# Attention into a mixture of experts on one core: which DMA engines carry the rows of one weight, and how the output's first tiles are split

## The chip, the core and the metric

The kernel runs on one core of a Trainium2 chip. The core has TensorE (PE) for matrix products, VectorE (DVE) and ScalarE (ACT) for elementwise work, GpSimd (POOL) and SyncE (SP), which issue transfers here, and sixteen DMA engines that move the data. The metric is the time of one execution on the device in microseconds. Times are medians over runs; a profiled execution gives the details.

## The reference

Attention over 4 batches of 8 heads (768 positions, 64 columns), with a causal mask that in some heads keeps only the first 4 positions and a window of 64. Its output, as 3072 rows of 512, goes through a soft mixture of 8 experts with 4 slots each:

```python
a = softmax(where(mask, q @ k.T / 8, -1e9)); x = a @ v      # 3072 x 512 over all heads
logits = x @ phi                                           # 3072 x 32
d = exp(logits) / sum over rows; slot_input = d.T @ x      # 32 x 512
for e in range(8):
    slot_out[e] = maximum(slot_input[e] @ w1[e], 0) @ w2[e]
c = exp(logits) / sum over slots
out = c @ slot_out                                         # 3072 x 512, float32
```

Inputs and output are float32; the kernel works in bfloat16 between them. The sixteen weights (eight w1, eight w2) are 2 MB each in float32.

## The kernel before

The instruction order comes from a planner that is part of the kernel: `pl.op` registers an operation with the engines that may run it, an estimated duration, a due time and what it depends on, and `pl.run()` places all operations in one order from these; each engine's queue holds its operations in that order. What the planner thinks of durations has no part in the time on the chip except through the order.

**Loads.** All of q, k, v and all weights (except a first slice of weight 0, and phi) are loaded by GpSimd (`dma`, line 281; the issue is line 283), with a cast from float32 to bfloat16 on the way. The order of the loads is written out by hand (line 901). A load waits for the landing of the load eight places before it. A weight takes a tile of 128 partitions; one row of it, 4096 numbers, is 16 KB in DRAM and 8 KB in the tile. Weight 5 is `UNEVEN` (line 355): it is loaded in five pieces of 112, 5, 5, 5 and 1 rows, each issued in turn. It lies in the middle of the load order, before the last parts of q, k and v and the ten weights after it. The last weight, number 15, is loaded in two halves of 256 columns each, `w15a` and `w15b`, so that the work on the first half can begin before the second is there.

**The tail.** After attention, the products with w1 (`H`, line 945) and w2 (`W2`, line 990) follow each other as the weights land. The products of the last w2 are done for columns 0 to 255 (`W2.7`, when `w15a` is there) and later for columns 256 to 511 (`W2.8`, when `w15b` is there). The accumulated slots are scaled by the reciprocal of a sum: `SOa` (line 1008) writes the first half, on ScalarE, `SOc` copies it on GpSimd into the tile that holds both halves, and `SOb` (line 1013) writes the second half; it may go to ScalarE or VectorE, and the planner puts it on ScalarE.

**The output.** It has 24 tiles of 128 rows by 512 columns (six groups `gi` of four, `r`). Each needs one product with the slots (`OM`, line 1056), and one scaling from PSUM into SBUF (`OE`, lines 1064 on ScalarE and 1066 on VectorE). The first six tiles (`half`, line 1044) are split by columns: their first halves need only `SOa` and are made while `w15b` is still being loaded, alternately on ScalarE and VectorE; their second halves need `SOb`. The remaining eighteen are made whole. The early products take turns on four PSUM banks. An extra dependency (lines 1073 to 1077) keeps `W2.8` behind the last early product in TensorE's queue.

**The stores.** SP issues eleven stores in the order of `store_parts` (line 1078): the first halves of tiles 0.0-0.1, 0.2-0.3 and 1.0-1.1, the second halves of the same, then tiles 1.2-1.3 whole, then four groups of four tiles (1 MB each). A store waits for the scalings of its tiles. A store of half tiles moves rows of 1 KB, the store of tiles 1.2-1.3 rows of 4 KB, the stores of groups rows of 8 KB.

Of the kernel before, what the change touches and what calls it, by code (L numbers as in the profile page):

```python
# [15 lines left out]
ACT = mybir.ActivationFunctionType  # L16
# [157 lines left out]
def kernel(  # L174
# [76 lines left out]
    def tr_bf(s, n):  # L251
# [17 lines left out]
    pl = Plan({"S8": 11, "QT": 2, "KT": 2, "VT": 1, "VB": 2, "VF": 3, "PT": 2, "PTX": 2, "XB": 2,  # L269
               "XT": 1, "SC": 2, "TR": 2, "PV": 1})  # L270
# [10 lines left out]
    def dma(name, key, nbytes, ndesc, buf, dst, src, deps=()):  # L281
        iss = pl.op("issue " + name, {"POOL": 0.62}, key, deps=deps, acq=[buf] if buf else [], lead=1.3,
                    emit=lambda o: nc.gpsimd.dma_start(dst(), src))  # L283
        issues.append(iss)
        gen = pl.op("gen " + name, {"GEN": 2.5 if name[0] == "w" and int(name[1:3].rstrip("abc")) > 5 else 1.45}, key, deps=[iss])
        land = pl.op("land " + name, {"DMA": dma_us(nbytes, ndesc) + LATE.get(name, 0.0)}, key, deps=[gen], lead=3.3)
        ring.setdefault(name, []).append((iss, land))
        return land

    def dma_us(nbytes, ndesc):  # L290
        return ndesc / 16 * 0.004 + nbytes / 16 / RATE
# [40 lines left out]
    def w_view(i):  # L332
        m = late_mem[i]() if i in late_mem else slots[wbuf[i].slot][:, :]
        return m.rearrange("p (a f) -> p a f", a=4 if i < NE else 8)

    def load_w(i, key, deps=()):
        if i == 0:

            flat = lambda: w_view(0).rearrange("p a f -> p (a f)")
            wland[0] = dma("w0", key, 7 << 18, 128, wbuf[0], lambda: flat()[:, WF:],  # L340
                           moe_w1[0].rearrange("(di do) f -> di (do f)", do=4)[:, WF:])
            w_cast.append(pl.op("CW", {"ACT": 0.6}, -90, deps=[wf_land], need=[wbuf[0]],
                                emit=lambda o: nc.scalar.copy(flat()[:, 0:WF], wf)))
            return
        if i < NE:
            src = moe_w1[i].rearrange("(di do) f -> di do f", do=4)
        else:
            src = moe_w2[i - NE].rearrange("(fi fo) d -> fi fo d", fo=8)
            if i == NW - 1:
                for k, (c0, c1) in enumerate(((0, CH), (CH, 512))):  # L350
                    last_lands.append(dma(f"w15{'ab'[k]}", key + 0.1 * k, (c1 - c0) << 12, 1024, None,
                                          lambda c0=c0, c1=c1: w_view(i)[:, :, c0:c1], src[:, :, c0:c1], deps=deps))
                wland[i] = last_lands[0]
                return
        if i == UNEVEN:

            buf, prev, land = wbuf[i], [], []
            for p0, p1 in ((0, 112), (112, 117), (117, 122), (122, 127), (127, 128)):
                land.append(dma(f"w{i}", key, (p1 - p0) << 14, p1 - p0, None if prev else buf,
                                lambda p0=p0, p1=p1: w_view(i)[p0:p1], src[p0:p1], deps=prev))  # L360
                prev = [issues[-1]]
            wland[i] = pl.op(f"landed w{i}", {"SP": 0.01}, key, deps=land)
            return
        wland[i] = dma(f"w{i}", key, 2 << 20, 128, None if i in late_mem else wbuf[i],
                       lambda: w_view(i), src, deps=deps)
# [151 lines left out]


    load_w(0, -30)
    for x in "ABC":  # L520
        load_tile(x, -29)
    load_w(1, -28)
    load_w(2, -27)
    for x in "DE":
        load_tile(x, -26)
# [103 lines left out]
    def evs(x, b, n):  # L629
        if b == 0:  # L630
            return ev[x, b]
        return [e for r0, r1, e in ev[x, b] if r0 < 24 * (n + 1) and r1 > 24 * n]
# [33 lines left out]
    for b in range(B):  # L666
        for n in range(4):
# [30 lines left out]
            for kk, g in enumerate(GORDER):  # L698
                sc = Buf("SC")
                key = k0 + kk * T / 5.3  # L700
# [17 lines left out]
                if g in (1, 3, 4):  # L718
                    m = {1: 0, 3: 1, 4: 2}[g]
                    masko[p, m] = pl.op(f"MK.{p}.{m}", {"DVE": [0.70, 0.70, 0.57][m]}, key + 0.3,  # L720
                                        deps=[expo[p, x] for x in ((0, 1), (2, 3), (3, 4))[m]] + o_hm[n],
                                        emit=mask_emit(b, n, m))

        for ns in ([(0, 1), (2, 3)] if b == 0 else [(0, 1, 2, 3)]):
            sc = Buf("SC")

            def emit_lx(o, b=b, sc=sc, ns=ns):
                sc_mms(sc, b, [(128 * x, n, XJ, XI, 1) for x, n in enumerate(ns)])

            key = T * (4 * b + ns[0]) + 0.9 * T  # L730
            a = pl.op(f"QX.{b}.{ns[0]}", {"PE": 0.09 * len(ns)}, key - 2.0, n=2 * len(ns),
                      deps=list(dict.fromkeys(e for n in ns for x in "qk" for e in evs(x, b, n))),
# [15 lines left out]
    for b in range(B):  # L748
        for n in range(4):
# [5 lines left out]
            for i in iorder:  # L755
                deps, need = [v2e[p], vfo[p]], set()
# [6 lines left out]
                def emit_pv(o, b=b, n=n, p=p, i=i):  # L763
                    pT = pTs[PTb[b, n].slot]
                    vb = vbs[VBb[b].slot]
                    for h in range(2):
                        for j in range(i + 1):
# [3 lines left out]
                            else:  # L771
# [5 lines left out]
                             deps=list(dict.fromkeys(deps)) + ([last] if last else []),  # L777
                             acq=[PVb[p]] if i == 0 else [],
                             rel=[PTb[b, n]] + ([VFb[p]] if i == 5 else []) +
# [72 lines left out]
        def emit_sa(o, b=b, dp=dp):  # L852
# [5 lines left out]
            else:  # L858
# [7 lines left out]
                       rel=[dp], emit=emit_sa)  # L866
# [47 lines left out]
    kt = T * 16 + 10  # L914
# [19 lines left out]
    hse, hte, w2o = {}, {}, []  # L934

    for e4 in range(2):
        hse[e4] = []
        for c in range(2):
# [13 lines left out]
            def emit_hr(o, e4=e4, c=c, bank=bank):  # L952
# [3 lines left out]
                else:  # L956
# [3 lines left out]
                                 rel=[hp], emit=emit_hr))  # L960
# [14 lines left out]
    so = Buf("PV")  # L975
# [26 lines left out]
    def emit_so(o, d, c0, c1):  # L1002
        if o.eng == "ACT":
            nc.scalar.activation(d[:, c0:c1], pvb[:, 0, c0:c1], ACT.Copy, scale=rcs[:, 0:1])  # L1004
        else:
            nc.vector.tensor_scalar(d[:, c0:c1], pvb[:, 0, c0:c1], rcs[:, 0:1], None, op0=ALU.mult)
# [3 lines left out]

    so_c = pl.op("SOc", {"POOL": 0.4}, kt + 20, deps=[so_a],
                 emit=lambda o: nc.gpsimd.tensor_copy(slot_out[:, 0:CH], slot_out_a[:, 0:CH]))
    so_b = pl.op("SOb", {"ACT": 0.46, "DVE": 0.49}, kt + 29.0, deps=[w2o[-1], so_c], rel=[so],
                 emit=lambda o: emit_so(o, slot_out, CH, 512))

    def emit_gz(o):
# [23 lines left out]
    def ot_view(gi):  # L1040
        return slots[wbuf[gi].slot].bitcast(F32)[:, :].rearrange("p (r d) -> p r d", r=4)

    oe, tiles = {}, [(gi, r) for gi in range(6) for r in range(4)]
    half = tiles[:6]
    parts = [(gi, r, 0, CH) for gi, r in half] + [(gi, r, CH, 512) for gi, r in half] + \
        [(gi, r, 0, 512) for gi, r in tiles[6:]]
    for m, (gi, r, d0, d1) in enumerate(parts):
        early = d0 == 0 and d1 == CH
        c = ("SC", "TR")[m % 2] if early else ("SC", "TR", "PV", "SC", "TR")[(m - len(half)) % 5]
# [5 lines left out]
        def emit_om(o, gi=gi, r=r, d0=d0, d1=d1, bank=bank, early=early):  # L1055
# [3 lines left out]
                  deps=[so_a if early else so_b], acq=[bf], emit=emit_om)  # L1059

        def emit_oe(o, gi=gi, r=r, d0=d0, d1=d1, bank=bank):
# [3 lines left out]
            else:  # L1065
                nc.vector.tensor_scalar(d, bank(), sc_, None, op0=ALU.mult)  # L1066

        w = (d1 - d0) / 512
# [7 lines left out]
    y.ndep += 1  # L1076
    x.succ.append(y)
    store_parts = [(gi, r0, r1, d0, d1) for d0, d1 in ((0, CH), (CH, 512)) for gi, r0, r1 in
                   ((0, 0, 2), (0, 2, 4), (1, 0, 2))] + [(1, 2, 4, 0, 512)] + [(gi, 0, 4, 0, 512) for gi in range(2, 6)]
    for n, (gi, r0, r1, d0, d1) in enumerate(store_parts):  # L1080
        def emit_st(o, gi=gi, r0=r0, r1=r1, d0=d0, d1=d1):
            dst = out[512 * gi:512 * (gi + 1), :].rearrange("(p r) d -> p r d", r=4)
# [25 lines left out]
    for o in order:  # L1108
# [9 lines left out]
        if front:  # L1118
# [3 lines left out]
            n = int(0.75 * (gap - 0.1) / unit + 0.5) if gap > 0.2 else 0  # L1122
# [23 lines left out]
        us, w = gap - (1.5 if o.name[:2] == "W2" else 0.12), 512 - c0  # L1146
# [53 lines left out]
```

## Time and profile before

| | us |
|---|---|
| median of 3 runs (range) | 148.75 (148.67 to 149.09) |
| profiled execution, whole time | 148.61 |
| its span, first to last instruction | 146.84 |
| PE, DVE, ACT busy in the span | 125.4, 111.6, 110.3 |
| load queue (q0), share of 16 engines over the span | 88.8% |

The times in the profile count from the first instruction of the span. "Busy" is the time in which an engine's instructions ran. The profile's DMA share is the mean busy share of the sixteen DMA engines; it can come out a little above 1 where the records of packets overlap. A load or a store is split into packets that the sixteen engines work through; each engine reports its part of a transfer as complete on its own, and the transfer has landed with the sixteenth report.

### The profile page before, as it was taken

How to read it: one execution, taken by the hardware profiler on the slowest of the kernel's cores; microseconds unless marked ns; L12 is line 12 of the kernel's file. 1: busy time of each engine (PE TensorE's matmuls, PEld its weight loads, DVE VectorE, ACT ScalarE, POOL GpSimd, SP SyncE). 2: the span in 40 equal slices, each digit the busy share in tenths (PEclk: the TensorE clock that was granted, in tenths of full speed). 3: DMA queues.
4: the chain of work that ended last, by engine and by line, in shares of the span. 5: the costliest groups of instructions: out<-in, count | busy, mean ns of one | idle time of the engine just before them, and what ended most of it. 6: DMA issues, size and time to landing. Idle time of an engine off the chain costs nothing.

```text
span 146.8 us, 4972 instructions
## 1 busy us (share of the span) xinstructions
PE 125.4 (85%) x2171; PEld 80.9 (55%) x2171; DVE 111.6 (76%) x244; ACT 110.3 (75%) x143; POOL 24.0 (16%) x48
## 2 busy tenths in 40 slices
PE   6999899989899998999999999998778996679200
PEld 2365566668576675877576776765534564233000
DVE  3898399987999899899999999999847610249500
ACT  3374999989999999999998999999814700469600
POOL 6921110412011211110400211010700000100000
PEclk9999999999999999999999999999999999968955
DMA  4999999999999999999999999999999999979996
GB/s 100 190 214 215 225 204 211 218 210 228 214 206 212 215 223 214 219 214 203 211 216 224 212 214 219 216 216 214 214 219 214 216 215 186 137 246 392 413 415 250
DMA packets 9608, 33.03 MB, mean 225 GB/s; under 512 B 867, under 2 KB 4595, under 8 KB 7283
## 3 DMA queue, kind: packets, MB, share of 16 engines
q0 software_dynamic: 6912, 26.09, 88.8%
q1 hardware_dynamic: 2672, 6.62, 11.8%
q8 instruction: 17, 0.28, 0.7%
q14 instruction: 5, 0.04, 0.1%
q10 hardware_dynamic: 2, 0.00, 0.0%
HBM read 52.49 MB, written 6.29 MB: 400 GB/s over the span
## 4 chain that ended last, share of the span: by engine, by line
DMA 33%; PE 23%; DVE 15%; ACT 14%; POOL 4%; issue 4%; ACTq 0%; POOLq 0%
DMA slot<-in_v_dram 17%; DMA qk<-in_moe_w_dram 16%; ACT pt L713 9%; PE pv L773 7%; PE sc L641 6%; DVE pt L658 4%; DVE xv L787 3%; POOL slot L283 3%; PE tr L611 3%; DVE qk L278 2%; ACT slot L1064 2%; PE tr L799 2%; DVE xT L278 2%; PE tr L676 2%; PE sc L1056 1%
## 5 line engine op out<-in xcount | busy, mean ns | idle before, releaser
L713 ACT ACTIVATE pt<-sc 128x1024 bf16<-128x1024 f32 x80 | 76.8, 1045 | 3.0 <-PE sc L641 2.5
L641 PE MATMUL sc<-qk 64*128 64x512 bf16 (+3 forms) x256 | 31.2, 308 | 2.7 <-ACT pt L713 1.8
L658 DVE TENSOR_TENSOR pt<-pt,msk 128x1024 bf16<-128x1024 bf16 (+1 forms) x48 | 30.0, 640 | 0.5 <-ACT pt L713 0.4
L773 PEld LDWEIGHTS <-pt 128*128 128x128 bf16 x640 | 23.4, 97 | 6.7 <-issue 5.6
L773 PE MATMUL pv<-vx,pt 128*128 128x65 bf16 x352 | 26.1, 193 | 0.1
L773 PE MATMUL pv<-vf,pt 128*128 128x65 bf16 x288 | 20.9, 194 | 0.0
L641 PEld LDWEIGHTS <-qk 64*128 64x128 bf16 x256 | 10.3, 93 | 11.5 <-issue 4.5
L611 PE MATMUL tr<-ident,slot 128*64 128x128 bf16 (+1 forms) x448 | 15.5, 219 | 0.5 <-DMA slot<-in_v_dram 0.5
L787 DVE TENSOR_TENSOR xv<-pv,rs 128x768 bf16<-128x768 f32 x16 | 15.3, 957 | 0.6
L611 PEld LDWEIGHTS <-slot 128*64 128x64 bf16 (+1 forms) x448 | 12.7, 110 | 3.6 <-issue 3.2
L283 POOL DMA_DIRECT2D slot<-in_moe_w_dram x15 | 8.1, 541 | 39.8 <-PE tr L611 9.1
L278 DVE COPY qk<-tr 128x768 bf16<-128x768 bf16 (+2 forms) x24 | 12.9, 551 | 0.7 <-PE tr L611 0.4
L278 DVE COPY xv<-tr 128x768 bf16<-128x768 bf16 (+2 forms) x20 | 8.4, 432 | 2.9 <-PE tr L569 2.9
L799 PE MATMUL tr<-ident,xv 128*128 128x128 bf16 x96 | 8.1, 220 | 2.2 <-DVE xv L787 1.9
L278 DVE COPY xT<-tr 128x768 bf16<-128x768 bf16 x14 | 7.8, 554 | 1.0 <-PE tr L799 0.8
L1004 ACT ACTIVATE msk<-pv,rcs 128x256 bf16<-128x256 f32 x2 | 0.9, 474 | 10.0 <-PE pv L990 10.0
L799 PEld LDWEIGHTS <-xv 128*128 128x128 bf16 x96 | 5.7, 97 | 4.7 <-DVE xv L787 2.2
L1066 DVE TENSOR_SCALAR slot<-tr,rrow 128x256 f32<-128x256 f32 (+1 forms) x6 | 3.3, 571 | 6.5 <-PE tr L1056 6.4
L676 PE MATMUL tr<-ident,xv 128*128 128x128 bf16 x96 | 7.9, 220 | 0.1
L278 DVE COPY vx<-tr 128x768 bf16<-128x768 bf16 x14 | 7.7, 550 | 0.2 <-PE tr L676 0.2
L1157 PE MATMUL pv<-zero 128*128 128x512 bf16 x30 | 7.5, 382 | 0.0
L692 DVE TENSOR_TENSOR vf<-vx,fm 128x528 bf16<-128x528 bf16 x16 | 6.9, 430 | 0.3
(122 smaller groups left out, 172.3 us busy)
## 6 DMA issues: line engine op xcount, KB each, us to landing
slot<-in_moe_w_dram POOLq DMA_DIRECT2D x9, 1024.0 KB, 22.8
out_dram<-slot SPq DMA_DIRECT2D x4, 1024.0 KB, 5.9
slot<-in_q_dram POOLq DMA_DIRECT2D x3, 768.0 KB, 20.0
slot<-in_k_dram POOLq DMA_DIRECT2D x3, 768.0 KB, 15.1
slot<-in_moe_w_dram POOLq DMA_DIRECT2D x2, 896.0 KB, 23.1
slot<-in_v_dram POOLq DMA_DIRECT2D x2, 768.0 KB, 13.2
out_dram<-slot SPq DMA_DIRECT2D x6, 256.0 KB, 2.5
slot<-in_v_dram POOLq DMA_DIRECT2D x2, 512.0 KB, 24.2
```

Source lines behind the costliest of these rows:

```text
L278: nc.vector.tensor_copy(dst, src)
L283: emit=lambda o: nc.gpsimd.dma_start(dst(), src))
L611: nc.tensor.transpose(t[64 * i:64 * (i + 1), :, s, :], rv[:, i, 8 * c + s, :], ident[0:nr, 0:nr])
L641: nc.tensor.matmul(scb[sc.slot][:, i, c:c + 128 * nb], kk, qq.rearrange("p b c -> p (b c)"), start=True, stop=True)
L658: nc.vector.tensor_tensor(pw, pw, mw, op=ALU.mult)
L676: nc.tensor.transpose(t[:, 128 * j:128 * (j + 1)], vT[:, 6 * n + j, :], ident)
L692: nc.vector.tensor_tensor(vfs[VFb[p].slot], vv, fm[:, n], op=ALU.mult)
L713: nc.scalar.activation(pTs[PTb[b, n].slot][:, :, 512 * g:512 * (g + 1)], scb[sc.slot], ACT.Exp, scale=scale)
L773: nc.tensor.matmul(pvb[:, h, 65 * i:65 * (i + 1)], lt, rhs, start=(j == 0), stop=(j == i))
L787: nc.vector.tensor_tensor(xo, pvw[:, :, :, 0:64], r.rearrange("p i (j o) -> p i j o", o=1).to_broadcast([P, 2, 6, 64]), op=ALU.mult)
L799: nc.tensor.transpose(t[:, 128 * i:128 * (i + 1)], xv[:, i, 128 * n:128 * (n + 1)], ident)
L1157: nc.tensor.matmul(bank[:, c0:c0 + w], zero[:, 0:128], zero[:, 0:w], start=(c0 == 0), stop=True, skip_group_check=True)
```

## The change

Two things are changed. Weight 5 is loaded in pieces of 96, 8, 8, 8 and 8 rows; the second piece takes 8 consecutive rows (96 to 103), the last three take every third row from 104, 105 and 106 on. And the output's first seven tiles, instead of six, are split by columns; the third and the sixth store now hold three half tiles each (1.0 to 1.2), and the seventh store holds tile 1.3 alone. `SOb` may only go to VectorE.

```diff
         if i == UNEVEN:

             buf, prev, land = wbuf[i], [], []
-            for p0, p1 in ((0, 112), (112, 117), (117, 122), (122, 127), (127, 128)):
-                land.append(dma(f"w{i}", key, (p1 - p0) << 14, p1 - p0, None if prev else buf,
-                                lambda p0=p0, p1=p1: w_view(i)[p0:p1], src[p0:p1], deps=prev))
+            for p0, p1, st in ((0, 96, 1), (96, 104, 1), (104, 128, 3), (105, 128, 3), (106, 128, 3)):
+                n = len(range(p0, p1, st))
+                land.append(dma(f"w{i}", key, n << 14, n, None if prev else buf,
+                                lambda p0=p0, p1=p1, st=st: w_view(i)[p0:p1:st], src[p0:p1:st], deps=prev))
                 prev = [issues[-1]]
...
-    so_b = pl.op("SOb", {"ACT": 0.46, "DVE": 0.49}, kt + 29.0, deps=[w2o[-1], so_c], rel=[so],
+    so_b = pl.op("SOb", {"DVE": 0.49}, kt + 29.0, deps=[w2o[-1], so_c], rel=[so],
                  emit=lambda o: emit_so(o, slot_out, CH, 512))
...
-    half = tiles[:6]
+    half = tiles[:7]
     parts = [(gi, r, 0, CH) for gi, r in half] + [(gi, r, CH, 512) for gi, r in half] + \
-        [(gi, r, 0, 512) for gi, r in tiles[6:]]
+        [(gi, r, 0, 512) for gi, r in tiles[7:]]
...
     store_parts = [(gi, r0, r1, d0, d1) for d0, d1 in ((0, CH), (CH, 512)) for gi, r0, r1 in
-                   ((0, 0, 2), (0, 2, 4), (1, 0, 2))] + [(1, 2, 4, 0, 512)] + [(gi, 0, 4, 0, 512) for gi in range(2, 6)]
+                   ((0, 0, 2), (0, 2, 4), (1, 0, 3))] + [(1, 3, 4, 0, 512)] + [(gi, 0, 4, 0, 512) for gi in range(2, 6)]
```

In the built program the engines' instructions are the same up to the tail. There, TensorE has one product of 256 columns more ahead of `W2.8`; ScalarE has the first half of tile 1.2 in the place of `SOb`; VectorE has `SOb` behind its three early halves; after `SOb` the weight load of the next product waits for VectorE; and the scalings that follow are shared out with a few tiles exchanged between the two engines. GpSimd and SP issue as many transfers as before, in the same order.

## The prediction

> **What bounds the kernel now.** I read the chain that ended last first. From 31 to 104 us it runs through ScalarE, VectorE and TensorE, but its last load is another matter:
>
> ```profile
> 105.17 23.61 DMA qk<-in_moe_w_dram
> 128.78 0.04 issue
> 128.82 0.43 PE pv L990 x8
> ...
> 129.27 0.48 ACT msk L1004
> 129.75 0.04 issue
> 129.79 0.32 PE sc L1056
> ```
>
> The second half of the last weight takes 23.61 us from issue to landing because it queues behind other loads. From 5 us on the page's windows show a DMA share of 1.0 or more, so the loads are one stream, and its end (128.78) is set by the DMA engine with the most work. The queue part of the page names what else these engines carry:
>
> ```profile
> q0 software_dynamic: 6912, 26.09, 88.8%
> ...
> q8 instruction: 17, 0.28, 0.7%
> q14 instruction: 5, 0.04, 0.1%
> ```
>
> Next I took the trace's completions, sixteen for each load, one per engine. The last half weight completes at 125.67, 125.72 and 126.05 on three engines, at 127.67 to 128.36 on twelve, and at 128.78 on one. So three engines idle for some 2.7 us while one works. Followed packet by packet, the reason is this. A row of a weight occupies an engine for 0.606 us (start to start). Each 16 KB instruction packet (0.89 to 1.03 us) holds up one engine, and where I could follow them it was always one of the same eight: from weight to weight an engine's completion moves by 4.85 to 4.90 us, and by 0.95 to 1.04 more with a packet. By 117.0 the eight **heavy** engines have had two each, about 1.9 us; the eight **light** ones none. The three 5-row pieces of weight 5 went whole, row by row, to the same five light engines (15 rows start there at 67.42 to 69.55). Those five carry 10 1/16 rows of this weight, the others 7 1/16, and 3 x 0.606 = 1.82 us offsets the 1.9. Three light engines were left out. The engine that ends last is one of the five: at 80.04 an 8 KB packet of queue 14 (322 ns, and 838 instead of 625 ns for the row behind it) put it 0.53 us behind.
>
> Then the tail, in windows (PE, PEld, DVE, ACT, POOL busy, clock, DMA share, GB/s):
>
> ```profile
> 127.00:128.00 1.00, 0.64 (x5) 0.42 (x5) 0.46 (x2) 0.64 (x3) 0.40 (x1) 1.00 0.87 124
> 128.00:129.00 1.00, 0.53 (x10) 0.27 (x9) 0.87 (x3) 0.74 (x2) 0.00 (x0) 1.00 0.07 13
> 129.00:130.00 1.00, 0.43 (x10) 0.28 (x3) 0.00 (x0) 0.47 (x1) 0.00 (x0) 0.94 0.84 269
> 130.00:131.00 1.00, 1.00 (x7) 0.60 (x6) 0.63 (x2) 0.84 (x2) 0.00 (x0) 0.50 1.03 343
> 131.00:132.00 1.00, 1.00 (x4) 0.42 (x4) 0.70 (x2) 0.83 (x3) 0.00 (x0) 0.50 0.69 235
> 132.00:133.00 1.00, 1.00 (x4) 0.29 (x2) 0.82 (x2) 0.83 (x2) 0.00 (x0) 0.50 1.03 336
> 138.00:142.00 4.00, 0.00 (x0) 0.00 (x0) 0.00 (x0) 0.09 (x1) 0.00 (x0) 0.76 1.01 418
> ```
>
> The stores start at 129.05, end at 145.57, and 1.27 us later the span ends. In between the queue is full except for 0.08 us near 129.8 and the 0.31 us that the share of 0.69 shows in 131 to 132: the three early stores are out by 131.62 and the fourth, waiting for the late half, begins at 131.81. So the time is: landing of the last weight's **first** half (126.11) + 2.94 us to the first store packet + the stores' own time + gaps.
>
> **Weight 5.** Five issues stay five on POOL (about 0.5 us each, none waits on new work), all bytes stay. The piece of 96 rows gives six rows to each engine, as 112 gave seven. What the others give is not in the trace, so both ends:
> - *Halves.* The 8 consecutive rows are cut over all sixteen engines, half a row each, as the single row was (its sixteen 512-byte packets stand in the trace); the three strided pieces give a row each to eight engines, the light ones. Light 9.5, heavy 6.5. The five and the heavy ones lose 0.56 rows (-0.34 us); the three gain 2.44 rows (1.48 us, to 127.53). The last completion goes from 128.78 to 128.44: **-0.34 us**.
> - *Whole.* All four pieces give whole rows to the light eight: 10 and 6. The five lose 1/16 row (-0.04), the three gain 2.94 (1.78, to 127.83), the heavy lose 1.06 (-0.64, to 127.72). The last engine is one of the five, so 128.74: **-0.04 us**.
>
> For whole rows speaks that five consecutive rows stayed whole; for halves, that five cannot be cut into sixteen equal parts while one row and eight rows can. The built program writes the single row as 16 pieces and the eight as 8 rows, which leaves it open. I take halves, by a little. The first half weight ends on the same engine, so it moves as much, and with it the early products and stores.
>
> **The seventh early tile.** One more product of 256 columns on TensorE (early ones start 0.10 us apart), one more scaling on ScalarE. The timeline has the early scalings:
>
> ```profile
> 127.44 1.31 ACT L1064 ACTIVATE slot<-sc,rrow 128x256 f32<-128x256 f32 x3 [0.36 <-PE sc L1056]
> ...
> 127.54 1.33 DVE L1066 TENSOR_SCALAR slot<-tr,rrow 128x256 f32<-128x256 f32 x3 [4.87 <-PE tr L1056]
> ```
>
> The product needs the bank that ScalarE's second scaling frees at 128.28, so it runs by 128.6; the last weight's products behind it in TensorE's queue started at 128.82, so it hides (up to 0.1 us if not). ScalarE's fourth scaling ends at 128.75 + 0.47 = 129.22. The third store waits for it, but SP was busy with the second store until 129.42 and issued the third at 129.52: hidden. That store grows from 256 to 384 KB, 0.77 to 1.16 us, so it ends at 132.0, past the fourth store's 131.81. The gap of 0.31 us closes: **-0.31**. The price: in 1 KB rows 256 KB keep the engines 0.77 to 0.81 us, in 4 KB rows 1.31 us per 512 KB, 0.655 per 256; a tile more in halves costs +0.12. The tile left over goes out in 2 KB rows, which no store shows; between 4 KB and 1 KB rows it costs 0 to 0.07, I take 0.01. Together **+0.13**.
>
> **The slots' second scaling on VectorE.** It has ended its early work by 128.87, so it is free at 129.25; a VectorE scaling of this shape takes 475 to 484 ns, ScalarE's took 474: +0.01. Left on ScalarE it would stand behind the fourth early scaling (129.22), almost no difference. But in the new order the weight load of the next product, and not only the product, waits for VectorE; after the one such wait in the trace (130.91 to 130.98) the product came 0.07 us later. So up to +0.1 on the way to the fourth store: 131.9 instead of 131.81, still covered by the longer third store. If that cover fails, it costs these 0.1. The eighth store (issued 134.44, first packet 135.40, while the seventh ended at 135.55) has little room too: TensorE has 256 columns less to do before it, about 0.2 us at the clock of 0.50, which pays for the 0.1.
>
> **Sum.** -0.34 - 0.31 + 0.13 = -0.52 us against the profiled execution's 148.61 (span 146.84), so 148.09; the median of the runs shown is 0.14 higher, so **148.25** in median. With whole rows: -0.04 - 0.31 + 0.13 = -0.22, 148.5.
>
> **Rivals.**
> 1. *Whole rows* (above): 148.5. Chance 0.34.
> 2. *Alternating eights:* each 8-row piece takes the next eight engines. Then all carry 8 rows, and the heavy gain 0.94 rows (0.57 us): the latest of them, 128.36, becomes 128.93, 0.15 later than now; with the tail's 0.18 the time is the same, 148.7. Against it: the three 5-row pieces did not move on. Chance 0.07. The Trainium skill (DMA: Bandwidth & Descriptors, Why a DMA increments its semaphore by 16 and not by 1) has such a rule, k consecutive engines from a round-robin cursor, beside an exception that gives one row per engine from the first on; the trace's 5-row pieces agree with the exception.
> 3. *Slower, the rows fall on the heavy eight.* If the step of three partitions, and not only the number of rows, picks the engines, the strided pieces can land on the heavy ones: 9.5 rows there, 2.44 x 0.606 = 1.48 us more, 129.84 instead of 128.78: +1.06 - 0.18, so 149.6. It decides once the heavy ones get over a row more than today's 7 1/16 (128.36 + 0.61 - 0.18 is 128.79). Against it: starts at partitions 112, 117 and 122 gave the same five engines. Chance 0.12.
> 4. *It buys nothing:* the last loads are held up elsewhere (an instruction packet on an engine that is not yet done; one started at 127.96) and the smaller packets cost their 0.13: 148.9. Chance 0.05.
>
> **How the numbers follow.** Halves have 0.42. A measurement of this kernel tells about 0.3%, 0.45 us, from no change, so faster means under 148.3. Halves, with 148.25 and some 0.1 on the edits that are hidden, share their 0.42 as 0.32 faster, 0.08 same, 0.02 slower, because the tail's covers can also turn out better when the stores begin earlier; whole rows as 0.08, 0.24, 0.02; alternating 0.01, 0.05, 0.01; rival 3 0.12 slower; rival 4 0.01, 0.01, 0.03. Together 0.42 faster, 0.38 same, 0.20 slower. The range of 147.9 to 149.1 holds the first, the second, alternating and nearly all of rival 4; of the low end, 148.1 has the gap closed with no price for the packets, and 0.2 is for the runs' own spread.
>
> **What would show it.** Halves: sixteen more 4 KB packets on the load queue near 68 us, all sixteen completions of the last half weight within 1.3 us and the last near 128.4. Whole rows: 8 KB packets only, heavy engines done a good 0.6 us earlier, the last near 128.7. The tail: a DMA share of 1.0 in 131 to 132, four early scalings on ScalarE ending before the third store's issue, L1007 on VectorE at about 0.48 us. Wrong if the last landing comes after 128.9 or if the gap in the stores only moves.

## The result: 0.8% slower, and the profile after

The changed kernel takes 149.93 us (median of 4 runs, 149.77 to 150.04), the kernel before 148.71 (148.55 to 149.09) beside it: a ratio of 1.0078, 95% interval 1.0059 to 1.0096, or 1.2 us more. The prediction said 148.25 and 147.9 to 149.1. The profiled execution took 149.99 us, its span is 148.18.

The chain that ended last, read as before (start, length, what):

```profile
104.97 25.07 DMA qk<-in_moe_w_dram
130.04 0.04 issue
130.08 0.43 PE pv L991 x8
...
130.61 0.50 DVE msk L1007
131.10 0.05 issue
131.15 0.40 PE sc L1057
```

The second half of the last weight lands at 130.04, not at 128.78: 1.26 us later. Its sixteen completions, one per engine, stand in the trace:

| | sixteen completions of the last half weight, us |
|---|---|
| before | 125.67 125.72 126.05, twelve from 127.67 to 128.36, 128.78 |
| after | 125.07 125.17, twelve from 127.23 to 128.56, **129.63 130.04** |

The twelve in the middle moved little; two engines fell 1.1 and 1.5 us behind the last of the twelve, and two now wait some 4.9 us at the end. The first half weight's last completion moved in the same way, 126.11 to 127.39, the first store packet from 129.05 to 130.33, the last store's end from 145.57 to 146.84. So the whole loss is there when the first half weight has landed; from there on the two kernels take the same time. The queues confirm that it isn't more data but idle engines (packets, MB, share of sixteen engines' span; before 88.8%):

```profile
q0 software_dynamic: 6896, 26.09, 87.9%
...
q8 instruction: 17, 0.28, 0.7%
q14 instruction: 6, 0.04, 0.1%
```

The packets of weight 5, followed engine by engine, tell which rows went where. None is cut: no 4 KB packets come in beside the other loads' own. All four pieces of 8 rows put one row on each of the **same** eight engines (their first rows start at 66.91 to 67.53 on six and at 68.00 and 68.41 on two). Six of the eight are light. The other two are heavy ones, about 1 us behind when the rows come. And two light engines got nothing: their part of the weight was over at 66.99 and 67.13.

The windows of the tail (PE, PEld, DVE, ACT, POOL busy, clock, DMA share, GB/s):

```profile
127.00:128.00 1.00, 0.41 (x9) 0.24 (x9) 0.00 (x0) 0.12 (x1) 0.00 (x0) 1.00 0.56 75
128.00:129.00 1.00, 0.59 (x4) 0.38 (x4) 0.17 (x1) 0.64 (x2) 0.40 (x1) 1.00 0.27 45
129.00:130.00 1.00, 0.64 (x4) 0.28 (x3) 1.00 (x3) 1.00 (x4) 0.00 (x0) 1.00 0.12 19
130.00:131.00 1.00, 0.40 (x8) 0.12 (x7) 0.55 (x2) 0.39 (x2) 0.00 (x0) 0.99 0.64 210
131.00:132.00 1.00, 0.85 (x5) 0.61 (x6) 0.29 (x2) 0.42 (x1) 0.00 (x0) 0.50 0.97 318
132.00:133.00 1.00, 1.00 (x5) 0.52 (x4) 1.00 (x3) 1.00 (x4) 0.00 (x0) 0.50 1.02 349
133.00:134.00 1.00, 1.00 (x4) 0.40 (x3) 0.84 (x2) 0.62 (x2) 0.00 (x0) 0.50 0.89 287
```

Read the share column. In before it fell below a third for one window only; here it is 0.27 and 0.12 for two, while a few engines finish the loads. The hole in the stores (0.69, in 131 to 132, in before) is smaller and lies elsewhere (0.89, in 133 to 134), and the scalings run as drawn up: four early ones on ScalarE, `SOb` on VectorE.

### The profile page after: what moved, and what is told of

Its sections match the earlier page's. It is cut to its first block, busy times and chain, and to the rows that moved or that the text cites. A ratio compares the mean times of both kernels' runs of the same rounds, so it can differ in the third digit from the quotient of the medians.

```text
span 148.2 us, 4977 instructions
## 1 busy us (share of the span) xinstructions
PE 124.6 (84%) x2172; PEld 80.6 (54%) x2172; DVE 112.4 (76%) x245; ACT 109.8 (74%) x143; POOL 23.9 (16%) x48
## 4 chain that ended last, share of the span: by engine, by line
DMA 33%; PE 22%; DVE 16%; ACT 13%; POOL 4%; issue 4%; ACTq 0%; POOLq 0%; DVEq 0%
DMA qk<-in_moe_w_dram 17%; DMA slot<-in_v_dram 16%; ACT pt L714 9%; PE pv L774 7%; PE sc L642 6%; DVE pt L659 4%; DVE xv L788 3%; POOL slot L283 3%; PE tr L612 3%; DVE qk L278 2%; ACT slot L1065 2%; PE tr L800 2%; PE sc L1057 2%; DVE xT L278 2%; PE tr L677 1%
## 5 line engine op out<-in xcount | busy, mean ns | idle before, releaser
L1067 DVE TENSOR_SCALAR slot<-tr,rrow 128x256 f32<-128x256 f32 (+1 forms) x8 | 4.5, 613 | 6.3 <-PE tr L1057 6.2
```

## Experiments

The theory, **T1**: a piece of n rows, with n up to 16, goes whole, one row per engine, always to the first n engines of one fixed order. The first five of these are light, of the next three two are heavy, so pieces of 8 rows load two heavy engines; this is all of the loss, and the tail is worth little. The rivals: **R1**, the step of three partitions picks the engines; **R2**, the tail lost the time.

**Either half of the change alone.** The first kernel is before with only the last three hunks of the diff, the second has only the first hunk.

> Weight 5 in the five pieces of before (112, 5, 5, 5, 1 rows), the tail of after: seven tiles in halves, the slots' second scaling on VectorE. T1 (the weight's rows lost the time, the tail gained and lost the same): the last half weight's last completion stays near 128.78 and the median is within 0.15 us of before, 148.6 to 148.85. R2 (the tail change lost the time): 149.9. The prediction's tail (-0.31 + 0.13): 148.55, with the gap in the stores of 131 to 132 gone; by T1 the gap moves to 132 to 134 and the stores' busy time grows by 0.17.

> Weight 5 in the five pieces of after (96 rows, 8, and three of 8 with a step of three), the tail of before: six tiles in halves, scaling left to the planner's choice. T1: the last half weight's last two completions near 129.6 and 130.0 as in after (before: 128.78), so 149.9 (+1.2). R2 (the tail change lost the time): 148.7 or less.

Measured: tail alone 148.63 against 148.87, ratio 0.9986 (0.9971 to 1.0002); rows alone 150.04, ratio 1.0080 (1.0063 to 1.0097). The rows have all of it, and R2 falls. The chain of the second kernel shows the late landing with the old tail:

```profile
106.05 24.43 DMA qk<-in_moe_w_dram
130.48 0.04 issue
130.53 0.43 PE pv L991 x8
```

Its last completions are 128.26, 129.15, 129.33 and 130.48, its first 124.90 and 125.45: the picture of after, with one engine more behind 129.

**No step.** After, with consecutive rows in all pieces:

```diff
-            for p0, p1, st in ((0, 96, 1), (96, 104, 1), (104, 128, 3), (105, 128, 3), (106, 128, 3)):
+            for p0, p1, st in ((0, 96, 1), (96, 104, 1), (104, 112, 1), (112, 120, 1), (120, 128, 1)):
```

> After, with the last three pieces of weight 5 as consecutive rows (104 to 111, 112 to 119, 120 to 127) instead of every third row. T1 (the number of rows picks the engines: eight rows always go to the same eight, two of them heavy): nothing changes, last completion near 130.0, 149.9. R1 (the step of three partitions picks the engines): consecutive rows go elsewhere, the last completion falls to 128.4 to 128.8 and the time to 148.2 to 148.7. Halves of rows, if a consecutive piece is cut: 4 KB packets near 68 us and about 148.4.

Measured: 150.10, ratio 1.0079 (1.0061 to 1.0098), as after. Last completions 128.83, 130.12 and 130.13, first 125.14 and 125.84. With or without the step the time and the picture are the same: R1 falls.

**Other sizes.** Before, with pieces that differ in size:

```diff
-            for p0, p1 in ((0, 112), (112, 117), (117, 122), (122, 127), (127, 128)):
+            for p0, p1 in ((0, 96), (96, 102), (102, 109), (109, 118), (118, 128)):
```

> Tail of before; weight 5 in pieces of 96, 6, 7, 9 and 10 rows, to see which engines a small piece picks. T1 (a piece of n rows puts one row on each of the first n engines): of the four small pieces the first six engines get 4 rows, the seventh 3, the eighth and ninth 2, the tenth 1, the other six none. Then the heavy engine among the first eight that is seventh or eighth shows by its 3 or 2 rows; engines with 10 and 9 rows that are heavy end past 129, others not. Time between 148.7 and 150. Rival (the pieces walk on from where the last one stopped): 32 rows fall evenly, two each, no engine has more than two whole rows of these pieces, about 148.9.

Measured: 149.42 in one run. Matched from load to load, six engines take 2.5 to 2.7 us from their completion of the first piece to that of the last (four rows of 0.606 us are 2.42), one takes 1.85 (three rows, 1.82), two 1.0 and 1.6, the other seven 0.6 to some 0.75. Six engines with four rows and one with three are what T1 says; below that the match is too coarse. (The same count of engines with four rows is eight in after and in the two kernels above.) Last completions: 125.34, 126.17 and 126.30; ten from 127.29 to 128.09; 128.72, 129.13, 129.71. So three light engines are left with few rows, five light ones are among the six, and the sixth is a heavy one, the latest:

```profile
105.26 24.45 DMA qk<-in_moe_w_dram
129.71 0.04 issue
129.76 0.43 PE pv L990 x8
```

An even spread of the 32 rows, the rival, has no place for three engines behind 128.7 and one at 125.34. A second kernel goes higher, with pieces of 80, 10, 11, 13 and 14 rows:

> Tail of before; weight 5 in pieces of 80, 10, 11, 13 and 14 rows. T1 (a piece of n rows puts one row on each of the first n engines): five rows each from the first piece, and from the small ones 4 on the first ten engines, 3 on the eleventh, 2 on the next two, 1 on the fourteenth, none on the last two. With seven light and three heavy engines among the first ten (from the sizes before: five light, two heavy, a light one, and one of each behind) three heavy engines have 9 rows, 1.94 more than before, and end at 128.9 to 129.5; the light ones with 9 rows end near 127.0, and the latest landing is 0.1 to 0.7 later than 128.78, the time 148.9 to 149.5. Rival (small pieces fall evenly): 8 rows on each engine, as with one piece of 128: heavy ones near 128.3 to 128.9, light ones at 126.2 to 126.8, and no engine beyond 129.

Measured: 149.18 in one run, and three engines from 128.89 to 129.44 (128.89, 129.11, 129.44), as T1 said; the slackest ends at 124.55. One engine behind 129 would not decide it alone, since a kernel with even rows has one too (129.45, below); but its earliest engine ends at 126.20, and one at 124.55 has fewer rows than an even spread gives. The engines between were not told apart one by one, so the order is inferred from counts and completions: five light ones first, then a heavy one, six light among eight; three heavy among ten is what fits. The Trainium skill (DMA: Bandwidth & Descriptors, Why a DMA increments its semaphore by 16 and not by 1) has both rules that the prediction named: engines taken from a cursor that moves on, and, as an exception on trn2, ceil(partitions / 16) rows per engine beginning at the first. These runs agree with the exception for the small pieces that were tried, 5 to 14 rows, and nothing in them shows a moving cursor; the single row of before is cut over all sixteen engines.

**Half the dose, and none.** Two pieces of 8 rows instead of four (112, 8, 8), and one piece of 128:

> Tail of before, weight 5 in 112 rows and two pieces of 8: half the dose of after. T1: the two heavy engines among the first eight have 9 rows, 1.94 more than before, 1.18 us; in before they ended near 127.9 and 128.3 (after's 129.63 and 130.04 less 2.94 rows), so the last completion comes at 129.0 to 129.45, +0.3 to +0.7, and the time is 149.2 to 149.6. Rival (any piece of eight rows costs a fixed delay): +0.6 or nothing, and the heavy engines end with the others.

> Tail of before, weight 5 as one piece of 128 rows: eight rows on every engine, one issue instead of five. T1 (the end is that of the engine with the most rows plus its instruction packets): the heavy engines have 8 instead of 7 1/16 rows, so the latest of them goes from 128.36 to 128.93, and the light ones all end near 126.3 to 126.8; the time is 0.1 to 0.2 above before. Rival (the rows of weight 5 don't set the end, only the pieces' own waits do): fewer pieces, so the same or faster, 148.6 to 148.8, with the light engines not earlier.

Measured: two pieces of eight 148.95, ratio 1.0023 (1.0004 to 1.0042); one piece 149.17, ratio 1.0032 (1.0012 to 1.0052). With two pieces the last completions are 128.98, 129.07 and 129.11, in the expected place; but T1 has two engines there, and what holds the third was not followed. The time is below the 149.2 to 149.6 that was expected; as a difference, some 0.3 us, it is at the low end (0.3 to 0.7):

```profile
105.54 23.57 DMA qk<-in_moe_w_dram
129.11 0.04 issue
```

With one piece seven engines end at 126.20 to 126.82 and one at 127.24, the eight light ones; the others at 128.29 to 128.84 and one at 129.45. The split in two groups is there, and 128.84 is near what was expected of the latest (128.93); but one engine comes 0.6 us behind it, which T1 does not explain and which was not followed, and with it the loss is 0.5 us instead of 0.1 to 0.2. So the five pieces of before do earn their place: without them the kernel is slower, by 0.2 to 0.8 us.

**A finer levelling, which failed.** The tail of after; the third piece of 5 rows and the single row behind it become six single rows, since a single row is cut over all sixteen engines. Against before, the loop over the pieces is

```diff
-            for p0, p1 in ((0, 112), (112, 117), (117, 122), (122, 127), (127, 128)):
+            for p0, p1 in ((0, 112), (112, 117), (117, 122)) + tuple((p, p + 1) for p in range(122, 128)):
```

> Tail of after; weight 5 in 112 rows, two pieces of 5 and six single rows, eight issues more than two pieces would need. T1: a single row is cut over all sixteen, so the five light engines have 9 3/8 rows instead of 10 1/16 (-0.42 us, the latest 128.36) and the heavy ones 7 3/8 instead of 7 1/16 (+0.19, the latest 128.55): the last completion falls by 0.2 to 128.55, and the time is 0.2 below that of the tail of after alone, a ratio of about 0.9973 to before. Rival (the single rows' small packets and the three more issues on POOL, 0.5 us each, cost as much): no gain, 0.9986 or above.

(Nine issues, four more than before; the text says three.) Measured: 153.65, ratio 1.0331 (1.0310 to 1.0353), 5 us slower. Neither T1 nor its rival foresaw this. Windows of this kernel around weight 5, columns as above:

```profile
65.00:70.00 5.00, 5.00 (x115) 3.84 (x115) 4.97 (x11) 4.95 (x6) 0.49 (x1) 1.00 0.80 157
70.00:75.00 5.00, 4.96 (x78) 2.84 (x75) 4.90 (x10) 5.00 (x7) 3.91 (x7) 1.00 0.51 70
```

The DMA engines run dry: 0.51 in 70 to 75, where before has 1.07. In 60 to 80 us GpSimd's queue waits 14.1 us in both kernels, here for landings alone, in before 4.1 for a landing and 10.0 for TensorE. What differs is what has been issued by then. The load of q that follows weight 5 goes out at 71.6 us in this kernel and at 55.9 in before (duration in ns as minimum, median and maximum, then first and last start):

```profile
L283 POOL DMA_DIRECT2D slot<-in_q_dram x1: 546/546/546, 71.6 to 71.6; - x1
```

```profile
L283 POOL DMA_DIRECT2D slot<-in_q_dram x1: 561/561/561, 55.9 to 55.9; - x1
```

A load waits for the landing of the load eight places before it. The ninth piece of weight 5 therefore waits until its first piece, the 112 rows, has landed, and then only eight small pieces are in flight, 16 rows in all: the engines have nothing left while the next loads are still being issued. The theory about the rows is not tested by this kernel; its cost is that of the places.

**The parts of the tail.** Seven tiles in halves, `SOb` kept on ScalarE (weight 5 as before):

```diff
-    so_b = pl.op("SOb", {"DVE": 0.49}, ...
+    so_b = pl.op("SOb", {"ACT": 0.46}, ...
```

> Weight 5 as before, seven tiles in halves as in after, but the slots' second scaling kept on ScalarE. It separates the two parts of the tail change. If VectorE's scaling or the wait of the weight load behind it costs something (0.1 to 0.2), this is faster than the tail of after alone: 0.1 to 0.2 us under its ratio of 0.9986, so about 0.998. If the scaling's place costs nothing, the ratio is again 0.9986, within its interval, and the fourth store is issued 2.1 to 2.2 us behind the last landing as in both. With ScalarE's fourth early scaling in its way (ends near 129.2) it could also be later by up to 0.2 where the last landing is early.

Measured: 148.54, ratio 0.9989 (0.9974 to 1.0003). Both tails were measured a second time:

> The tail of after alone, once more (ratio 0.9986, from 0.9971 to 1.0002, the first time), since 0.18 us is at the edge of what five rounds tell. The prediction's tail of -0.18 us is a ratio of 0.9988; the sum from the traces (first store packet to last store's end 16.52 in before, 16.45 in this kernel) is -0.07, 0.9995; no gain is 1.0.

> Seven tiles in halves with the slots' second scaling left on ScalarE, once more beside the tail of after (0.9989, from 0.9974 to 1.0003, the first time; first store packet to last store's end 16.33). If the scaling's place matters by the 0.1 us that the wait of the weight load could cost, this is 0.0005 to 0.001 below the other; if it is covered by the longer third store, the two agree within 0.0005.

Measured: `SOb` on VectorE 149.01, ratio 1.0032 (1.0003 to 1.0061); on ScalarE 148.67, ratio 1.0000 (0.9981 to 1.0020). The first of these kernels came out 0.2 us faster once and 0.5 us slower once (by the ratios): this spread is larger than the effect. What the traces can tell is the mechanism. First the chain with `SOb` on VectorE (tail alone), then with it on ScalarE:

```profile
128.89 0.43 PE pv L990 x8
...
129.42 0.50 DVE msk L1006
129.91 0.05 issue
129.96 0.30 PE sc L1056
```

```profile
128.75 0.43 PE pv L990 x8
129.18 0.02 issue
129.20 0.48 ACT msk L1004
129.69 0.04 issue
129.73 0.28 PE sc L1056
```

From the last weight's products to the first product of the second halves it takes 1.07 us with VectorE and 0.98 with ScalarE: 0.09 us is the price of the place. It shows again in both pairs of profiles: the fourth store is issued 2.09 and 2.08 us after the last landing with VectorE, 1.98 and 1.98 with ScalarE. And the hole of 131 to 132 closes with seven tiles, here with `SOb` on VectorE and then on ScalarE (share in the column before the last):

```profile
131.00:132.00 1.00, 1.00 (x6) 0.41 (x5) 1.00 (x3) 1.00 (x4) 0.00 (x0) 1.00 1.01 344
```

```profile
131.00:132.00 1.00, 1.00 (x5) 0.43 (x6) 1.00 (x3) 1.00 (x3) 0.00 (x0) 1.00 1.02 339
```

But a hole can open elsewhere. In the second profile of the tail of after alone the stores pause in 130 to 131 us; first the first profile, then the second:

```profile
130.00:131.00 1.00, 0.87 (x7) 0.55 (x7) 0.61 (x2) 0.72 (x2) 0.00 (x0) 1.00 0.93 307
```

```profile
130.00:131.00 1.00, 0.79 (x6) 0.57 (x7) 0.51 (x3) 0.59 (x2) 0.00 (x0) 1.00 0.53 169
```

SP took 1.25 us to issue the second store there, against 0.84 in the first profile and 0.79 in before, and the store's first packet came 1.35 us behind the first store's instead of 0.96 and 0.91. Why the issue took longer is not known.

From the first store packet to the last store's end, one value for each profile, by the granted clock in the tail and the kind of tail:

| granted clock | six tiles | seven, `SOb` on VectorE | seven, `SOb` on ScalarE |
|---|---|---|---|
| 1.00 throughout | 16.37, 16.38, 16.39, 16.40 | 16.45, 16.89 | 16.33, 16.57 |
| 0.50 for some 3 us | 16.52 (before), 16.38 | 16.52 (after), 16.50 | |

(The kernel of the finer levelling, with `SOb` on VectorE, has 17.07.) At a clock of 1.00 the profiles with the tail of after are longer than all with the old tail; at 0.50 they are as long as before's, or 0.02 us shorter, and longer than the other. So the times leave the tail's worth open, the mean of the two ratios being 1.0009 with `SOb` on VectorE and 0.9995 on ScalarE, and the profiles speak against the predicted -0.18 us. No version tried is faster than before beyond doubt.

## Why the prediction was wrong

- **The bound** was right: the time is the landing of the last weight's first half + 2.94 us + the stores. The 2.94 is the same in both kernels (126.11 to 129.05, 127.39 to 130.33), and the landing is that of the engine that is behind by the most rows and instruction packets.
- **The step that failed** is in both ends of the weight-5 part: "the three strided pieces give a row each to eight engines, the light ones" (halves) and "all four pieces give whole rows to the light eight" (whole). The trace of before showed five engines, all light, for pieces of five. I took from this that a piece seeks the light ones, where it only takes the first n of an order, and the first five happened to be light. Of the first eight, two are heavy. The term of -0.34 us (halves) or -0.04 (whole) came out as +1.26: with 10 rows instead of 7 1/16 these carry 2.94 x 0.606 = 1.78 us more; they ended at 129.63 and 130.04, so they would have ended at 127.85 and 128.26 in before, among its twelve (127.67 to 128.36). The price was right, the place was wrong.
- **Halves against whole:** whole rows, all four pieces. That 16 divides eight rows into halves was no reason; the trace of before had a reason on the other side, five whole rows.
- **Rival 3** (rows fall on the heavy engines, 149.6, chance 0.12) is nearest: 1.48 us for 2.44 rows. It was priced with the right formula and given the wrong condition, the step of three, which the kernel without the step shows to have no part in it. "The number of rows picks the engines, and not all of the first eight are light" was not among the cases.
- **Rival 2** (moving on by eights) fell: the four pieces have the same eight engines.
- **The tail**, -0.31 + 0.13 = -0.18, is not settled by the times, and the profiles speak against it. Some of its parts are seen: the longer third store covers the wait for the fourth, `SOb` takes 0.50 us, and the wait behind it costs 0.09 of the 0.1 allowed. The price of the packets was a little low: they take 16.27 us of the sixteen engines in after, 16.10 in before, +0.17 where +0.13 was said; the tile left over, in 2 KB rows, takes 0.69, 0.03 more than in 4 KB rows, where 0.01 was taken. And in after a hole remains, in 133 to 134 (0.89). What makes it was not isolated; the fourth store is issued 2.30 us after the last landing there, 2.14 in before. From the first store packet to the end of the seventh store it is 6.51 us in before and 6.46 in after: 0.05 of the 0.18.
- **What would show it:** "Wrong if the last landing comes after 128.9" was the first sign, and it came at 130.04. The second, "if the gap in the stores only moves", came in part: in after it moved and shrank. (148.09 + 0.14 is 148.23; the prediction rounds it to 148.25, and nothing hangs on that.)

## What to carry to other kernels

In this kernel a load of 5 to 14 rows is not spread: all that was seen fits one row on each of the first engines of a fixed order, so a second such load adds to the same engines. Before rows are moved to level the engines, find out from the completions which engines a piece of that very size takes; a smaller piece's engines don't tell it. And small pieces cost places in the window of loads in flight, which may be dearer than the unevenness that they cure (5 us here).

## What the hardware showed that was not expected

- Engines that got no 16 KB instruction packets and engines that got two each lie mixed in the order in which small transfers take them: five without, then one with, six without among the first eight, as the completions above let one infer.
- The granted TensorE clock fell to 0.50 for about 3 us in the tail of some executions (130 to 133 in before, 131 to 134 in after) and stayed at 1.00 in others (the four windows shown for the tails alone). A product of 128x512 takes 631 ns in 130 to 133 of before, and 378 in the kernel with the tail alone. The eighth store was issued 5.66 us after the last landing in before and 4.89 in the kernel with the tail alone, yet from the first store packet to the last store's end it took 16.52 and 16.45 us, since its packets queue behind the seventh's.
- SP's issue of the second store took from 0.41 to 1.25 us in the profiles of these kernels, and the store's packets shift with it.
- The same kernel, measured twice against before, gave 0.9986 and 1.0032: 0.7 us apart, with intervals that just fail to meet. Differences of 0.2 us are not settled by either.
